# Attention and a two-layer MLP in one kernel: the second layer of batches 2 to 7 by seven block products per pair of tiles, with more key sums on TensorE

## The chip, the cores and the metric

The kernel runs on one core of a Trainium2 chip. The metric is the device time of one execution in microseconds (us). Engines are named as in the profile: PE is TensorE, PEld its weight loads, DVE is VectorE, ACT is ScalarE, POOL is GpSimd, and SP is SyncE, whose queue carries most DMAs. Each engine runs its own list of instructions in order, and waits at an instruction until what it needs is there.

## The reference

Eight batches of 12 heads, 448 tokens and 64 features go through attention with normalised queries and keys. The heads of a token are put side by side, which gives x with 3584 rows of 768, and two matrix products with a gelu between them follow.

```python
q_n, k_n = rmsnorm(q, g_q), rmsnorm(k, g_k)
scores = scale * np.matmul(q_n, k_n.transpose(0, 1, 3, 2))
scores = scores - np.max(scores, axis=-1, keepdims=True)
attn = np.exp(scores)
attn = attn / (np.sum(attn, axis=-1, keepdims=True) + 1e-09)
x = np.matmul(attn, v).transpose(0, 2, 1, 3).reshape(B * S, H * D)
h = x @ w_in                                   # 768 -> 2048
g = 0.5 * h * (1 + np.tanh(c * (h + 0.044715 * h * h * h)))
out = g @ w_out                                # 2048 -> 768
```

Inputs and outputs are float32; matmuls take bf16.

## The kernel before

**Work of a batch.** Queries and keys are loaded by SP in three chunks c of four heads (tiles `raw`). Their squares are made on ACT (L170) or POOL (L172), summed along the features on DVE (`total`, L177), and turned into reciprocal roots; `normed` (L279) multiplies, on POOL, six operations a batch. DMA transposes on SP (`dma_trans`) bring the result into `kT` and `qT`, and DVE applies the gains to `kT` (`gain`, L321).

An attention has 21 `unit`s: three chunks c times seven key tiles t. A unit is a round of four 64x64 matmuls with 448 columns (scores, L334) and an exp on ACT into the tile `ex` (L338). For the softmax's denominator the seven exps of a chunk are added on DVE in `key_sums` (L355 to L361: `es` = first two, then pairs `e2`, then `es` += `e2`), and the sum goes through one round with a matrix of ones on PE (`products(b, c, 0)`, L383). `added(b, c)` says up to which tile the exps are added first; all that are left would take a round each. `products(b, c, 1)` multiplies with v, seven rounds a chunk. `turned` (L392, two transposes of half a tile) and `recips` (L400 reciprocal, L401 transpose back) give `rb`, one over the denominators, and `quad_x` (L409) multiplies them with the product, into `xT`.

The first layer (`mm1_pair`, L599: 128x128 matmuls with 448 columns, 96 a batch, gelu on ACT at L612) writes `g`. The first two pairs of it begin, with the first two thirds of xT, at the end of the attention (the `m` steps), the rest follows. In the second layer (`mm2_quarters`, L443) a round is four 64x64 matmuls with 384 columns. Two products (a token tile of 128 by half of the 768 columns) share a PSUM pair `o`; each goes over the 16 blocks of the 2048 twice, in two phases p that use the opposite halves of the rows. Between the phases SP issues a `nop` (L452) that the next phase waits for, a "turn". Tiles are of 128 tokens of two batches together: an even batch gives three tiles, 96 rounds, an odd one four, 128 rounds. The four tiles of the last batch go through `quad_of_products` instead: the two tiles of a pair, the two halves of the 2048 and the two halves of the columns form 2x2 blocks, and seven products of block sums (L529, full 128x128 matmuls with 384 columns) give four blocks of output. The sums of g (`token_sums`, L517) and of the weights (`weight_sums`, L486) are made on DVE ahead of it.

**Order.** The order is written by hand and is the same on every engine's list. The first two batches are a string of steps (`first_two`). From then on the loop over b emits the first layer of batch b, with normalising of batch b+1 and loads and squares of batch b+2 put between its blocks by `plan` (`m1`), and then `attention(b + 1)`, whose string `steps` (one for even, one for odd) mixes U (a unit), d and a (rounds of the second layer of batch b; the copy that ends a product goes to DVE or ACT), A (key adds), s and x (`products`), t, r, q and m. I call such a stretch, first layer of b and attention of b+1, period b. The second layer's rounds come from a list that runs on from one period to the next, so each period has 112 of them. POOL's `mark` (`gpsimd_waits`, L756) copies one element of the last `es` of a batch; POOL's normalises of the next batch stand behind it.

**PSUM.** Four pairs of banks (s0, s1, t0, t1 in the names `s` and `t`) are handed out by `pair` and given back by `give`, first in, first out. A score, a product with v or ones, a first-layer pair and a second-layer product each take one.

**Buffers.** `rawqk` 4 of each, `sqp` 2 squares, `exq` 2 tiles of exps, `vb` 2 (v of even and of odd batches), `xp` 2, `op` 3 output tiles.

## Time and profile before

| what | value |
|---|---|
| median of 3 runs | 393.72 us (393.67 to 395.22) |
| the profiled execution | 394.05 us |
| its span in the profile | 392.1 us (1.95 us lie outside it) |
| mean granted clock of TensorE | 1.00 |
| second layer, L443 | 3072 matmuls, 768 rounds |
| scores L334, products L383 | 672 and 872 matmuls |
| first layer, L599 | 768 matmuls |
| POOL | 125.8 us busy in 105 instructions |

The span is the time from the profile's first instruction to its last. A row of the profile's groups has line, engine, operation, output and inputs with their shapes and a count, then busy time in us and the mean of one in ns, and behind a second bar the idle time of the engine ahead of them and what ended it. A row of the timeline has start, length, engine, line and operation; in square brackets the idle time before it. A row of the table by stretch has the stretch, its length and the busy time (and instructions) of PE, PEld, DVE, ACT and POOL, then PE's clock, DMA's share and GB/s.

### The profile page before, as it was taken

What the parts mean: (1) busy time and instruction counts of PE and PEld (TensorE: products, weight loads), DVE (VectorE), ACT (ScalarE), POOL (GpSimd) and SP (SyncE); (2) the same over time, 40 slices, a digit from 0 to 9 for tenths busy, and PEclk for the clock granted to TensorE, in tenths of its full rate; (3) what the DMA queues carried; (4) which work ended last, traced back from release to release, by engine and by line L of the source; (5) the groups of instructions that cost most, each with busy time, mean ns of one, the idle gap of its engine ahead of it and who ended that gap; (6) DMA issues with size and microseconds to landing.
All of it is one profiled execution on the core that took longest, in us unless ns stands there. A gap on an engine that the chain in (4) does not pass through costs nothing.

```text
span 392.1 us, 12742 instructions
## 1 busy us (share of the span) xinstructions
PE 384.0 (98%) x5649; PEld 245.3 (63%) x5649; DVE 271.9 (69%) x424; ACT 277.8 (71%) x349; POOL 125.8 (32%) x105
## 2 busy tenths in 40 slices
PE   7989999999999999999999999999999999999996
PEld 6455567855676558865666557865566556875554
DVE  4999539996699357963599456982579613999743
ACT  6995489567996589857898479857899349873410
POOL 5995501863304540083301840054400900000000
PEclk9999999999999999999999999999999999999999
DMA  8999997899752969249651859239632621120024
GB/s 266 255 233 222 204 186 153 303 185 260 150 135 56 249 81 225 55 98 272 106 144 42 192 137 205 65 86 230 118 75 46 132 47 43 43 57 27 0 61 101
DMA packets 65770, 54.36 MB, mean 139 GB/s; under 512 B 37428, under 2 KB 60852, under 8 KB 65716
## 3 DMA queue, kind: packets, MB, share of 16 engines
q1 hardware_dynamic: 53200, 41.33, 41.9%
q0 software_dynamic: 12128, 11.80, 19.4%
q8 instruction: 44, 0.72, 0.8%
q10 hardware_dynamic: 388, 0.43, 0.3%
q14 instruction: 10, 0.08, 0.1%
HBM read 45.61 MB, written 11.01 MB: 144 GB/s over the span
## 4 chain that ended last, share of the span: by engine, by line
PE 91%; ACT 5%; DVE 1%; DMA 1%; issue 0%; POOL 0%; ACTq 0%
PE s L599 21%; PE t L443 19%; PE t L599 15%; PE s L443 12%; PE s L383 6%; ACT ex L338 4%; PE s L334 4%; PE t L334 3%; PE t L383 3%; PE s L529 2%; PE t L529 2%; PE o L383 1%; PE tp L297 1%; DMA rawq<-in_q_dram 1%; PE hh L599 1%
## 5 line engine op out<-in xcount | busy, mean ns | idle before, releaser
L599 PEld LDWEIGHTS <-win 128*128 128x128 bf16 x768 | 74.4, 98 | 70.8 <-issue 2.6
L443 PEld LDWEIGHTS <-g 64*64 64x64 bf16 x3072 | 98.0, 107 | 32.8 <-SPq L452 2.9
L338 ACT ACTIVATE ex<-s,shift 128x896 bf16<-128x896 f32 x101 | 97.8, 1011 | 4.5 <-PE s L334 2.7
L443 PE MATMUL t<-wout,g 64*64 64x384 bf16 x1792 | 90.4, 323 | 0.0
L599 PE MATMUL s<-xT,win 128*128 128x448 bf16 x438 | 88.3, 353 | 0.0
L177 DVE TENSOR_REDUCE ss<-sq 128x14 f32<-128x896 f32 (+3 forms) x45 | 44.4, 997 | 48.1 <-ACT sq L170 42.9
L338 ACT ACTIVATE ex<-t,shift 128x896 bf16<-128x896 f32 x67 | 66.4, 1014 | 5.8 <-PE t L334 3.0
L612 ACT ACTIVATE g<-s 128x896 bf16<-128x896 f32 (+1 forms) x41 | 34.0, 835 | 48.5 <-PE s L599 48.5
L599 PE MATMUL t<-xT,win 128*128 128x448 bf16 x318 | 64.7, 353 | 0.0
L443 PE MATMUL s<-wout,g 64*64 64x384 bf16 x1280 | 64.6, 323 | 0.1
L612 ACT ACTIVATE g<-t 128x896 bf16<-128x896 f32 (+1 forms) x30 | 24.8, 829 | 26.3 <-PE t L599 26.3
L334 PE MATMUL s<-qT,kT 64*64 64x448 bf16 x404 | 37.6, 353 | 2.0 <-ACT ex L338 1.5
L756 POOL COPY mark<-es 1x1 bf16<-1x1 bf16 x5 | 0.9, 177 | 116.0 <-DVE es L357 116.0
L279 POOL TENSOR_TENSOR nrmk<-rawk,rinv 128x896 bf16<-128x896 f32 (+1 forms) x21 | 34.5, 1647 | 5.4 <-DVE o L246 5.4
L279 POOL TENSOR_TENSOR nrmq<-rawq,rinv 128x896 bf16<-128x896 f32 (+1 forms) x21 | 34.5, 1643 | 4.2 <-ACT rinv L209 2.9
L334 PEld LDWEIGHTS <-kT 64*64 64x64 bf16 x672 | 23.7, 106 | 14.7 <-issue 6.3
L172 POOL TENSOR_TENSOR sq<-rawq 128x896 f32<-128x896 f32 (+1 forms) x9 | 13.6, 1516 | 54.1 <-DVE ss L177 28.2
L383 PEld LDWEIGHTS <-vb 64*64 64x64 bf16 x672 | 22.9, 107 | 8.1 <-issue 0.3
L401 DVE STREAM_TRANSPOSE rb<-rc 128x896 f32<-128x896 f32 x24 | 26.7, 1112 | 0.8
L334 PE MATMUL t<-qT,kT 64*64 64x448 bf16 x268 | 24.1, 351 | 0.3 <-ACT ex L338 0.2
L360 DVE TENSOR_TENSOR e<-ex 128x896 bf16<-128x896 bf16 x33 | 20.0, 606 | 6.2 <-ACT ex L338 6.2
L383 PE MATMUL s<-ex,vb 64*64 64x448 bf16 x420 | 22.8, 349 | 0.0
(123 smaller groups left out, 404.2 us busy)
## 6 DMA issues: line engine op xcount, KB each, us to landing
rawk<-in_k_dram SPq DMA_DIRECT2D x23, 448.0 KB, 5.6
out_dram<-osb SPq DMA_DIRECT2D x52, 192.0 KB, 3.1
rawq<-in_q_dram SPq DMA_DIRECT2D x22, 448.0 KB, 4.8
vb<-in_v_dram POOLq DMA_DIRECT2D x8, 672.0 KB, 7.2
wout<-in_moe_w_out_dram POOLq DMA_DIRECT2D x2, 1536.0 KB, 23.4
win<-in_moe_w_in_dram POOLq DMA_DIRECT2D x6, 256.0 KB, 11.2
win<-in_moe_w_in_dram POOLq DMA_DIRECT2D x4, 384.0 KB, 13.4
rawq<-in_q_dram SPq DMA_DIRECT2D x3, 224.0 KB, 3.9
```

The source lines that it names most:

```text
L172: eng.tensor_mul(sq, raw, raw)
L177: nc.vector.reduce_sum(sss[b][:, c, "qk".index(n), hs, ts], squares(b, c, n, hs, ts), axis=AX.X)
L279: eng.tensor_mul(nrms[n, b, c][:, ts].rearrange("p t a d -> p a t d"), raws[n, b, c][:, :, ts], root[:, :, ts].to_broadcast([P, 2, m, D]),)
L334: nc.tensor.matmul(sc[r * R:(r + 1) * R, a, :S], kT[rs, c, t, r], qT[b][rs, c, :, r], start=True, stop=True,)
L338: nc.scalar.activation(ex[:, t], sc[:, :, :S], AF.Exp, scale=scale, bias=shift)
L360: nc.vector.tensor_add(e2, ex[:, t - 1], ex[:, t])
L383: nc.tensor.matmul(o[r][a * D:(a + 1) * D], vb[b % 2][rs, 2 * c + a, i] if what else ones[rs], es[i][rs, a], start=(i == 0), stop=(i == n ...
L401: nc.vector.transpose(rb.rearrange("p r s -> p (r s)"), rc.to_broadcast([128, 2 * S // 32, 32]))
L443: done = nc.tensor.matmul(o[c * R:(c + 1) * R, n, :HD], g[rs, f, i * 128 + c * R:i * 128 + (c + 1) * R], wout[rs, f, half * HD:(half + 1) ...
L529: nc.tensor.matmul(o[:, lo:hi], g_of(qd, m, f), w_of(m, f)[:, lo:hi], start=start and f == 0, stop=f == nh - 1, skip_group_check=True,)
L599: nc.tensor.matmul(h[j][:, :S] if type(h) is list else h[:, j, :S], win[:, c, f * 128:(f + 1) * 128], xT[b][:, c], start=(c == 0), stop=(c ...
L612: nc.scalar.activation(g[:, 2 * i + lo:2 * i + js[-1] + 1, (b % 2) * S:(b % 2 + 1) * S], h[:, lo:js[-1] + 1, :S], AF.Gelu_apprx_tanh)
```

## The change

**The second layer of batches 2 to 6** (`FAST = 2`) is made of block products over pairs of tiles, in rounds of four 64x64 matmuls as before. With A the two tiles by two halves of the 2048 (even and odd blocks of 128) and B the same halves by two halves of the columns, seven products m = "1" to "7" give the four output blocks; the sums they need share parts: `pair_sums` (two at a time, `wino_sum`, on DVE or POOL) and one in place in `g`; `tsum` holds four sums of the weights (`weight_sum`, eight operations in period 2, kept to the end). A product is 8 blocks long. In an odd batch both pairs of tiles go through a product side by side: seven products in two phases of eight, 112 rounds for 128. In an even batch one pair and a plain third tile make groups A to F: 88 rounds for 96. Products whose results go into two outputs stay in PSUM: P and R (later Q) are open at once, so a second-layer product holds two of the four PSUM pairs most of the time. `wino_done` copies a finished half into `oall4` (on DVE or ACT as the step says) or adds it to what is there (DVE). Between phases there is a turn as before. The last batch's four tiles go through `last_tiles` with the same sums: again 112 products, in the order of `TAIL`.

```diff
+    def wino_tiles(b):
+        return ((0, 1),) if b % 2 == 0 else ((3, 4), (5, 6))
+    def a_of(b, k, m, j):
+        t = wino_tiles(b)[k]
+        if m in "12":
+            return g[:, 2 * j + "12".index(m), t[0] * 128:(t[0] + 1) * 128]
+        if m == "4":
+            return g[:, 2 * j + 1, t[1] * 128:(t[1] + 1) * 128]
+        if m == "7":
+            return g[:, 2 * j, t[1] * 128:(t[1] + 1) * 128]
+        return pair_sums[:, wino_slots(b)[k], "536".index(m) // 2, j]
+    def wino_sum(b, k, i, part, eng):
...
+        dst, x, y, op = {
+            "1": (s1, g_part(t[1], 0, lo, n), g_part(t[1], 1, lo, n), ALU.add),
+            "2": (s2, s1, g_part(t[0], 0, lo, n), ALU.subtract),
+            "3": (g_part(t[1], 0, lo, n), g_part(t[0], 0, lo, n), g_part(t[1], 0, lo, n), ALU.subtract),
+            "4": (s1, g_part(t[0], 1, lo, n), s2, ALU.subtract),
+        }[i]
+        eng.tensor_tensor(dst, x, y, op=op)
+    def weight_sum(m, part, eng):
...
+        x, y, op = {"7": (b22, b12, ALU.subtract), "5": (b12, b11, ALU.subtract),
+                    "6": (own["7"], b11, ALU.add), "4": (b21, own["6"], ALU.subtract)}[m]
+        eng.tensor_tensor(own[m], x, y, op=op)
+    def wino_round(b, group, ph, j, copy):
...
+        for n in range(2):
+            lhs, rhs = two[n](j)
+            r = n ^ p
+            rs = slice(r * R, (r + 1) * R)
+            for c in range(2):
+                done = nc.tensor.matmul(
+                    o[c * R:(c + 1) * R, n, :HD], lhs[rs, c * R:(c + 1) * R], rhs[rs],
+                    start=firsts[n] and begins and j == 0, stop=swap == 1 and j == nh - 1,
+                    skip_group_check=True,
+                )
...
+            groups = [("1", "P", T, N), ("5", "R", T, N), ("6", "P", N, N), ("3", "R", N, T),
+                      ("7", "P", N, N), ("2", "Q", T, T), ("4", "P", N, T)]
...
+    TAIL = "1a 5a 6a 3a 7a 1b 4a 5b 6b 3b 7b 2a 4b 2b"
```

**Key sums.** `ADDED` lets more exps go to PE: batches 2 to 7 have 7 or more rounds of key sums where they had 3; with the first batches' that is 71 rounds for 50. The adds that are left are 81 on DVE (118 before) and 16 of the pairs `e2` on POOL ("Ap" in the strings). `turned` transposes a whole pair at once, 128x896, and `rb` takes the place of `st`.

```diff
-        return NT - 1 if b > 1 else (6, 4, 0)[c] if b else 0
+        return ADDED[b - 1][c] if b > 1 else (6, 4, 0)[c] if b else 0
...
-            nc.vector.tensor_add(e2, ex[:, t - 1], ex[:, t])
-            nc.vector.tensor_add(es, es, e2)
+            eng.tensor_add(e2, ex[:, t - 1], ex[:, t])
+            add(es, es, e2)
...
+        if whole:
+            nc.vector.transpose(st.rearrange("p r a b -> p (r a b)"), oas["o", 0][:, :, :S])
+            give(oas["o", 0])
+            return
...
-        rb = oas["rb"] = stp.tile([128, 2, S], F32, tag="rb", name="rb")
+        rb = oas["rb"] = oas["st"].rearrange("p r a b -> p (r a b)")
...
+    ADDED = {1: (6, 6, 6), 2: (5, 5, 3), 3: (5, 5, 4), 4: (6, 5, 3), 5: (5, 5, 4), 6: (6, 5, 3)}
```

**Order and buffers.** `plan`, `attention` and the loop's `m1` and `side` give way to one string for each period (`PERIODS`, played by `period`), in which every load, square, normalise, sum, gain and DMA transpose has its place too. Of period 6, from the last half pair of the first layer (h.7.1) to its end; U, d, a, A, s, x, t, r, q and m are as before, G a `wino_sum` (pair, sum, part, engine), gn a gain, dt a DMA transpose, V the load of v, w.e the mark:

```diff
+            "e.5 e.6 L.k.2 h.7.0 sq.k.2.P.0 to.k.0 L.q.1 G.0.1.0.V h.7.1 d sq.k.2.P.1 d2 L.q.2 dt.q.0 "
+            "d2 eE sq.q.1.P.0 d sq.q.1.P.1 d2 gn.2.V U to.k.1 U w.e sq.q.2.P U d dt.q.1 to.q.1 d "
+            "to.k.2 d2 G.0.1.1.V d to.q.2 d4 Ap d2 A d U d4 U G.0.2.2.V d Ap d U A d A d4 U A d3 A d2 "
+            "U Ap d3 G.0.4.0.V G.0.4.1.V d U d3 U d3 s.0 d t A d2 r G.0.3.2.P d U d dt.q.2 V A d2 Ap "
+            "d U d2 U d5 U d3 x.0 U A d2 q.0 Ap d U d4 Ap U d s.1 t d U A d A d5 a r U2 x.1 U d Ap Ap "
+            "d Ap q.1 d3 A d2 A a s.2 rE x.2 m.0 t r eG m.1 q.2 "
```

The steps L, sq and to in it would serve batch 8 and do nothing, as there are eight batches from 0 to 7. Sixteen rounds of batch 1 go over from period 1 to period 2; from then on odd periods have 112 rounds and even ones 88. `rawqk` has 3 buffers of each instead of 4, `sqp` is gone (`square_place`: squares lie in `tsum` for the first batches, then in a slot of the exps' ring `exq`), `xp` and `op` have 1, `vb` is a single tile. Some 24 half squares go from ACT to POOL. `released` and its two held tiles are gone.

**What that does to DVE's list.** From the attention of batch 6, before: one copy of a finished second-layer product (L457), key adds (L355 to L361), two half transposes and the reciprocals.

```order
L355 TENSOR_TENSOR es<-ex 128x896
L457 COPY osb<-t_885 128x768
L360 TENSOR_TENSOR e_5531<-ex 128x896
L361 TENSOR_TENSOR es<-es,e_5531 128x896
L360 TENSOR_TENSOR e_5542<-ex 128x896
L361 TENSOR_TENSOR es<-es,e_5542 128x896
L357 TENSOR_TENSOR es<-es,ex 128x896
L355 TENSOR_TENSOR es<-ex 128x896
L392 STREAM_TRANSPOSE st<-s_100 128x448 x2
L400 RECIPROCAL rc<-st 128x28
```

After, in the same attention from the first copy of a block product (L585) on; L556 is a sum of g, L395 to L400 are key adds, L197 sums squares.

```order
L585 COPY osb<-t_866 128x2x384
L556 TENSOR_TENSOR pair_sums<-pair_sums,g 128x1024
L395 TENSOR_TENSOR es<-ex 128x896
L197 TENSOR_REDUCE ss<-sq 128x14
L585 COPY osb<-s_97 128x2x384
L400 TENSOR_TENSOR es<-es 128x896
L556 TENSOR_TENSOR pair_sums<-g,pair_sums 128x512
L556 TENSOR_TENSOR pair_sums<-g,pair_sums 128x1024
L556 TENSOR_TENSOR pair_sums<-g,pair_sums 128x512
L399 TENSOR_TENSOR es<-ex 128x896
L400 TENSOR_TENSOR es<-es 128x896
L350 TENSOR_SCALAR kT<-kT,gcols 128x896
```

Fewer key adds stand between two transposes, and sums of g and copies or adds of block products stand there instead; a first L400 without an L399 adds a pair that POOL made.

**And to POOL's.** Before, the normalises of batch 7: the mark, which waits for the last `es` of batch 6, and behind it the six normalises.

```order
L756 COPY mark<-es 1x1
L279 TENSOR_TENSOR nrmq<-rawq,rinv 128x2x7x64
L279 TENSOR_TENSOR nrmk<-rawk,rinv 128x2x7x64
L279 TENSOR_TENSOR nrmq<-rawq,rinv 128x2x7x64
L279 TENSOR_TENSOR nrmk<-rawk,rinv 128x2x7x64
L279 TENSOR_TENSOR nrmq<-rawq,rinv 128x2x7x64
L279 TENSOR_TENSOR nrmk<-rawk,rinv 128x2x7x64
```

After, the end of batch 6's attention and the normalises of batch 7; L399 is the key add of a pair of exps.

```order
L556 TENSOR_TENSOR pair_sums<-pair_sums,g 128x512
L149 DMA vb<-in_v_dram 128x6x448
L399 TENSOR_TENSOR es<-ex 128x896 x2
L308 TENSOR_TENSOR nrmk<-rawk,rinv 128x2x7x64
L308 TENSOR_TENSOR nrmq<-rawq,rinv 128x2x7x64
L308 TENSOR_TENSOR nrmk<-rawk,rinv 128x2x7x64 x2
L308 TENSOR_TENSOR nrmq<-rawq,rinv 128x2x7x64 x2
L989 COPY mark<-es 1x1
L556 TENSOR_TENSOR g<-g 128x8x128
L149 DMA vb<-in_v_dram 128x6x448
L399 TENSOR_TENSOR es<-ex 128x896 x3
```

The mark has moved behind the normalises, and POOL has key adds and sums of g of its own between them.

529 lines of the change are left out of this document (298 added, 231 removed), and 70 rows, old and new, of tables (PERIODS, m2, steps).

## Prediction

> **What bounds the kernel now.** I read the page's busy line, slices and chain first, then the table by stretch, then the groups by form and the waits, and last the timeline of VectorE (DVE), ScalarE (ACT) and GpSimd (POOL) around one end of a batch. The page's first lines and the chain by engine:
>
> ```profile
> span 392.1 us, 12742 instructions
> PE 384.0 (98%) x5649; PEld 245.3 (63%) x5649; DVE 271.9 (69%) x424; ACT 277.8 (71%) x349; POOL 125.8 (32%) x105
> PE   7989999999999999999999999999999999999996
> PE 91%; ACT 5%; DVE 1%; DMA 1%; issue 0%; POOL 0%; ACTq 0%
> ```
>
> PE is busy in 98% of the span, and in all but three slices it is at nine tenths or more; 91% of the chain is its own work. So the time is a count of TensorE's matmuls times their pitch, plus its waits. Two whole periods (the first layer of one batch and the attention of the next), then one attention and the first layer behind it, in the table by stretch:
>
> ```profile
> 215.97:306.50 90.53, 90.53 (x1452) 58.30 (x1449) 61.02 (x88) 70.49 (x88) 28.66 (x21) 1.00 0.58 129
> ...
> 279.70:306.50 26.80, 26.80 (x628) 17.97 (x621) 21.30 (x33) 24.57 (x28) 3.15 (x5) 1.00 0.38 73
> 306.50:324.70 18.20, 18.20 (x100) 9.31 (x96) 5.39 (x7) 6.85 (x8) 8.05 (x5) 1.00 0.39 76
> ```
>
> The first number is the length, then PE, its weight loads, DVE, ACT, POOL. PE has no gap at a clock of 1.00, but the averages hide that DVE works unevenly: 21.30 of 26.80 us in an attention, 5.39 of 18.20 in a first layer. Its end of an attention is close: the last product that xT needs runs here, while PE does two early pairs (3.0 us from 306.50):
>
> ```profile
> 285.83 0.96 DVE L457 COPY osb<-t 128x768 f32<-128x768 f32 x1 [1.87 <-PE t L443]
> ...
> 308.26 1.09 DVE L409 TENSOR_TENSOR xT<-t,rb 128x896 bf16<-128x896 f32 x1
> ```
>
> It ends at 309.35, some 0.2 us before PE turns to it (306.50 + 3.03). DVE has little to spare there, though the share says 69%.
>
> **Second layer and key sums on PE.** Prices are in these pieces of the chain:
>
> ```profile
> 282.98 1.30 PE t L443 x32
> ...
> 293.11 1.32 PE s L383 x28
> ```
>
> A round is four matmuls. Eight second-layer rounds take 1.30 us, 0.1625 each; seven rounds of 448 columns take 1.32, 0.189 each. Batches 2 to 6 had 96, 128, 96, 128, 96 rounds and get 88, 112, 88, 112, 88: 56 fewer, 56 x 0.1625 = 9.10 us off the path. Batches 0 and 1 keep theirs, batch 7 keeps 112 large products. The key sums go from 50 rounds to 71: 21 x 0.189 = 3.97 us onto the path. The sum is **-5.13 us** while PE stays without gaps. That the change fails to do this is no case: the rounds are issued or not, and they are counted. Two periods of before hold 282 rounds of 448 columns (first layer counted in the same unit) and 224 of 384: 282 x 0.1892 + 224 x 0.1625 = 53.4 + 36.4 = 89.8 against 90.53 in the row above, so 0.39 us a period of small waits already hide in PE's busy time. I credit none of it as gain.
>
> **Turns.** Between the two phases of a product SP passes on a wait:
>
> ```profile
> PEld L443 <- SPq L452: 2.9, 10, 0.5
> ```
>
> It cost 2.9 us in ten waits in all. Afterwards there are as many turns or more, each covered by a score or key-sum round ahead of it; I take no change, bounds -1 to +1.
>
> **DVE's load.** Its prices:
>
> ```profile
> L357 DVE TENSOR_TENSOR es<-es,ex 128x896 bf16<-128x896 bf16 x32 | 20.0, 624 | 3.0
> L392 DVE STREAM_TRANSPOSE st<-t 128x448 f32<-128x448 f32 x28 | 16.5, 628 | 1.2 <-PE t L383 1.1
> L400 DVE RECIPROCAL rc<-st 128x28 f32<-128x28 f32 x24 | 7.9, 328 | 0.8
> L401 DVE STREAM_TRANSPOSE rb<-rc 128x896 f32<-128x896 f32 x24 | 26.7, 1112 | 0.8
> L409 DVE TENSOR_TENSOR xT<-s,rb 128x896 bf16<-128x896 f32 x15 | 16.3, 1087 | 1.2 <-PE s L383 0.8
> L457 DVE COPY osb<-t 128x768 f32<-128x768 f32 x6 | 5.7, 957 | 15.5 <-PE t L443 15.2 <-DMA rawq<-in_q_dram 0.3
> L517 DVE TENSOR_TENSOR asum<-g 128x512 bf16<-128x512 bf16 x16 | 5.5, 420 | 2.9 <-ACT g L612 2.9
> L517 DVE TENSOR_TENSOR asum<-g 128x1024 bf16<-128x1024 bf16 x2 | 1.3, 688 | 0.6 <-ACT g L612 0.6
> L177 DVE TENSOR_REDUCE ss<-sq 128x14 f32<-128x896 f32 x37 | 39.9, 1083 | 44.6 <-ACT sq L170 39.5 <-POOL sq L172 5.1
> 280.89 0.44 DVE L321 TENSOR_SCALAR kT<-kT,gcols 128x896 bf16<-128x896 bf16 x1
> ```
>
> For batch 6's attention before, from the copy at 285.83 to 309.35: 18 key adds of 0.62, one copy, six half transposes of 0.63, three each of 0.33, 1.11 and 1.09: 23.5 us of work in 23.52 us. So sums of mean durations are a fair measure of DVE when it runs without stop. After the change the list from the first second-layer product (ready behind 16 rounds and three scores, 16 x 0.1625 + 3 x 0.189 = 3.2 us) to the last xT is: 12 key adds 7.4; four pair sums of 512 and two of 1024, 1.7 + 1.4; five copies or adds of 768 columns 4.8; a reduce 1.1; a gain 0.4; three whole transposes at the price of L401 (1.11 against 2 x 0.63) 3.3; three reciprocals 1.0; three L401 3.3; three L409 3.3: 27.7 us. It ends at 3.2 + 27.7 = 30.9 us. PE has 112 rounds, 49 of 448 columns and the two early pairs: 18.2 + 9.3 + 3.0 = 30.5. So PE waits some 0.4 us. In an even batch's period the list has 11 key adds (6.8), sums 1.5, three copies of 384 at half of L457 (1.5), two adds of 384 (1.1, half of L409), two of 768 (1.9) and the same 10.9: 23.7 from 3.2 on, 26.9 against PE's 88 x 0.1625 + 49 x 0.189 + 3.0 = 26.6: 0.3 late. Taken 0.35 in each of the five periods of batches 2 to 6: **+1.75 us**; bounds 0 (work in a better place) and 1.0 each. The period of batch 2 also holds eight weight sums, at this price 7.6 us, half of them in a first layer, where DVE idles; the ten at the end of before go:
>
> ```profile
> L486 DVE TENSOR_TENSOR wsum<-wout 128x1536 bf16<-128x1536 bf16 x10 | 8.8, 951 | 0.0
> ```
>
> **Accumulators.** Two second-layer products are open at once, so two of four PSUM pairs are left for scores, v products and key sums, and a score waits for the exp of two before it. ACT's pitch and its present waits:
>
> ```profile
> 326.73 3.70 ACT L338 ACTIVATE ex<-s,shift 128x896 bf16<-128x896 f32 x4
> ACT ex L338 <- PE t L334: 3.0, 7, 0.6
> ```
>
> Exps come every 0.9 us; units stand mostly 0.7 us or more apart, so a pair can come 0.2 to 0.6 late. DVE, which is the later one, uses that time too, so it isn't counted twice: 0 taken, bound 0.8 in each of the three even periods. ACT itself gets lighter (some 24 half squares go to POOL, at 0.57 in the row below), so it isn't the next bound.
>
> ```profile
> L170 ACT ACTIVATE sq<-rawq 128x448 f32<-128x448 f32 x22 | 11.9, 570 | 0.6 <-DMA rawq<-in_q_dram 0.6
> L279 POOL TENSOR_TENSOR nrmk<-rawk,rinv 128x896 bf16<-128x896 f32 x20 | 33.7, 1687 | 5.4 <-DVE o L246 5.4
> POOL mark L756 <- DVE es L357: 116.0, 5, 23.7
> ```
>
> **POOL.** It takes sixteen key adds (at L279's 1.69 us), those squares and some pair sums; at 125.8 us busy before, it has room. The question is what it does beside DVE. Before, POOL stood 116.0 us behind the mark, until the last key add was through. Afterwards the mark stands behind the normalises of most periods, so they start beside the last key adds. What a POOL operation does to one of DVE's shows here; DVE's gains alone normally take 0.44:
>
> ```profile
> 311.08 1.68 POOL L279 TENSOR_TENSOR nrmq<-rawq,rinv 128x896 bf16<-128x896 f32 x1
> 312.73 1.83 POOL L279 TENSOR_TENSOR nrmk<-rawk,rinv 128x896 bf16<-128x896 f32 x1
> ...
> 311.50 1.51 DVE L321 TENSOR_SCALAR kT<-kT,gcols 128x896 bf16<-128x896 bf16 x1 [2.16 <-DMA kT<-nrmk]
> 314.05 0.76 DVE L321 TENSOR_SCALAR kT<-kT,gcols 128x896 bf16<-128x896 bf16 x1 [1.04 <-DMA kT<-nrmk]
> ```
>
> Both gains ended 0.25 us after the POOL operation in whose time they fell (312.76, 314.56). They lost 1.07 and 0.32, a mean of 0.70 us a meeting. Not everything suffers: this pair of DVE ran at its usual speed inside POOL's normalises of 304.48 to 309.46:
>
> ```profile
> 305.47 1.17 DVE L392 STREAM_TRANSPOSE st<-s 128x448 f32<-128x448 f32 x2
> 307.04 1.11 DVE L401 STREAM_TRANSPOSE rb<-rc 128x896 f32<-128x896 f32 x1
> ```
>
> Whether a key add suffers, no row shows: before, none runs beside POOL. The bounds are none and every POOL operation of the attention (some five a period, 25 x 0.70 = 17.5 us in five periods); I take the price of one meeting on the path in all, **+0.7**, since in the order DVE's transposes, reduces and reads of PSUM stand beside a good part of POOL's work. [...]
>
> **V and the tail.** One v buffer instead of two lets the load start only behind the last v product of the batch before, on POOL's queue:
>
> ```profile
> DMA to landing us min/median/max: 6.5/7.2/28.1
> ```
>
> In an even period it is issued behind a pair sum; 7.2 us later is 13 to 15 us, against the first v product at 13.3. I take 0, bounds 0 and 1 a period in two periods. Likewise three raw buffers for four, and squares that take a slot of the exp tiles: a load or an exp can come late by the part of an attention that isn't spare; 0 taken, and a place in the upper end of the range. The last four tiles keep 112 products; their sums of weights are done earlier, 0 taken, bounds -0.5 and +0.5.
>
> **The sum.** 393.72 - 5.13 + 1.75 + 0.7 = 391.0 us. The profiled run took 394.05 (392.1 of span and 1.95 outside), 0.33 above the median; by it the sum is 391.4.
>
> **Rivals.** *A meeting in every period.* If key adds suffer as the gains do, and one meeting falls on the path in each of the five periods, 5 x 0.70 = 3.5 replaces the 0.7: 393.8, no change. For it: DVE's list is as long as the period, so each loss goes on to PE. Against: the lists end only 0.3 to 0.4 us late, so one operation less on DVE in a period takes much of a loss back. Chance 0.24.
> *POOL and DVE hold each other off (the other side).* Two meetings a period on the path, one of a key add or pair sum with a POOL key add or square, one of the last key adds with the next batch's normalises, which the mark no longer holds back: 10 x 0.70 = 7.0, 393.72 - 5.13 + 1.75 + 7.0 = 397.3. It decides from (1.75 + x 0.70 = 5.13) five meetings on. For it: the gains' rows, and the trace of before, which keeps the two apart with its 116.0 us wait. Against: the transposes beside POOL at full speed. It shows first at the key sums ahead of a transpose and at the end of an attention. Chance 0.24. [...]
>
> **How the numbers follow.** 0.5% is 2.0 us, about what a measurement of this kernel can tell from no change. My forecast, 391.0, is faster; chance 0.52, with 388.6 (no lateness at all) to 391.7. It, and the two rivals, give the chances 0.52, 0.24, 0.24. The low end, 387.5, is 388.6 less half of the 0.39 us x 6 that hides before; the high end, 397.5, takes in both rivals' prices; more than ten meetings, some 1 in 8, are left out above it, and less below 387.5.
>
> **What would show it.** PE busy should fall to some 379 (384.0 - 5.1), DVE stay near 270 (37 key adds fewer, but more sums and adds out of PSUM), and POOL rise to some 185 (125.8 + 16 x 1.69 + 24 halves of that + a dozen pair sums of one each). Right: waits of PE for xT at the start of a first layer of about 0.4 us each, and key adds near 0.62. The first rival: one key add a period of 1.3 us or more. The second: the mean of key adds well above 0.62 and PE gaps over 1 us per period ahead of the key sums or the first layer. Wrong in another way: PE waits for exps or a pair of PSUM, or for v, each over 1 us a period.

## The result, and the profile after

The changed kernel takes 409.41 us (median of 4 runs, 407.24 to 410.9) against 394.29 (393.67 to 395.22) of the kernel before, measured beside it: a ratio of 1.037 with a 95% interval of 1.034 to 1.041. It is slower by 15 us; the forecast was 391.0 and its upper end 397.5. The profiled execution took 409.1 us. The page's first lines, answering to those of before:

```profile
span 407.3 us, 12496 instructions
PE 386.4 (95%) x5509; PEld 242.6 (60%) x5509; DVE 279.9 (69%) x406; ACT 264.8 (65%) x325; POOL 198.1 (49%) x153
PE   7989999999899999999989999999998999999795
PEclk9999999999999999999999999999999999999989
```

PE has 140 matmuls fewer (5649 to 5509: 56 rounds off and 21 on, of four each), as counted, but the share of its busy time went from 98% to 95%, and three things are new: eights in the middle, a hole near the end, and a clock below full there. So the question is which waits came in. (The forecast expected PE at some 379 us busy, DVE at 270 and POOL at 185. PE's busy time isn't work alone: in batch 7's attention below it is 24.93 us for 23.57 by count.) The table by stretch holds the six attentions of batches 2 to 7, cut where PE leaves one first layer and enters the next. Before, the first and the last of the six:

```profile
98.17:125.45 27.28, 27.28 (x630) 19.14 (x629) 22.29 (x34) 24.73 (x28) 5.84 (x6) 1.00 0.53 118
...
324.76:351.69 26.93, 26.93 (x629) 21.50 (x629) 20.95 (x32) 24.10 (x26) 0.00 (x0) 1.00 0.18 47
```

And after, those of batches 2, 4 and 7:

```profile
99.08:128.51 29.43, 27.45 (x629) 18.64 (x629) 23.31 (x33) 24.77 (x29) 15.08 (x12) 1.00 0.53 114
...
194.60:225.72 31.12, 28.59 (x646) 21.47 (x645) 26.17 (x39) 25.19 (x29) 9.32 (x7) 1.00 0.51 72
...
336.38:361.62 25.24, 24.93 (x549) 18.03 (x548) 20.01 (x31) 22.94 (x25) 8.66 (x5) 1.00 0.50 80
```

The first two numbers are length and busy PE. This table sets each length against its count of rounds, at the prediction's 0.1625 and 0.189 us:

| attention of batch | 2 | 3 | 4 | 5 | 6 | 7 | all |
|---|---|---|---|---|---|---|---|
| before: length | 27.28 | 26.93 | 27.07 | 26.93 | 27.07 | 26.93 | 162.2 |
| before: by count | 26.71 | 26.71 | 26.71 | 26.71 | 26.71 | 26.71 | 160.3 |
| after: length | 29.43 | 28.79 | 31.12 | 25.23 | 30.63 | 25.24 | 170.4 |
| after: by count | 26.71 | 26.20 | 27.47 | 23.57 | 27.47 | 23.57 | 155.0 |
| after: late | 2.7 | 2.6 | 3.7 | 1.7 | 3.2 | 1.7 | 15.5 |

By count the attentions lose 5.3 us, as forecast. They grew by 8.2, since PE came 15.5 us late in them where it had been 1.9 late. Batches 5 and 7, with 88 rounds, are the only ones that got shorter. The rest of the 15.2 us of span: 4.65 in the last product of the kernel (18.55 to 23.20), 0.9 up to the first layer of batch 1, 0.8 in that of batch 3, 0.6 behind the last matmul; what makes these three was not looked into. PE's waits by what released it:

```profile
PE t L683 <- DVE pair_sums L556: 3.0, 1, 3.0
PE t L625 <- SPq L633: 2.1, 2, 1.3
PE s L363 <- ACT ex L367: 2.0, 5, 0.6
PE s L625 <- issue: 1.7, 1, 1.7
PE s L363 <- DVE osb L508: 1.4, 1, 1.4
...
PE t L739 <- DVE xT L457: 0.2, 1, 0.2
```

The third row is nearly old: before the change PE waited 1.5 us, four times, for ACT's exps. The others are new. So there isn't one cause but several, each once or twice. The wait on which the forecast spent its largest term, for xT at the start of a first layer, is the last line: 0.2 us in all.

**The last product.** DVE and POOL share the sums of g there. The timeline of DVE, of POOL, and PE's first round behind them:

```profile
380.57 0.76 DVE L556 TENSOR_TENSOR pair_sums<-g 128x512 bf16<-128x512 bf16 x2 [16.02 <-ACT g L752]
381.85 1.38 DVE L556 TENSOR_TENSOR g<-g 128x512 bf16<-128x512 bf16 x1
383.15 1.37 DVE L556 TENSOR_TENSOR pair_sums<-pair_sums,g 128x512 bf16<-128x512 bf16 x1
...
384.44 2.67 DVE L556 TENSOR_TENSOR pair_sums<-g,pair_sums 128x512 bf16<-128x512 bf16 x2
```
```profile
381.48 1.47 POOL L556 TENSOR_TENSOR pair_sums<-pair_sums,g 128x512 bf16<-128x512 bf16 x1 [7.30 <-DVE pair_sums L556]
382.91 3.58 POOL L556 TENSOR_TENSOR g<-g 128x512 bf16<-128x512 bf16 x2
```
```profile
386.83 2.37 PE L683 MATMUL t<-wout,pair_sums 128*128 128x384 bf16 x8 [2.97 <-DVE pair_sums L556]
```

A sum of 512 columns took 0.38 us on DVE before POOL began (two in 0.76), and 1.38, 1.37 and 2.33 beside POOL; the last is the first of the two in 2.67, the second took 0.41 when POOL was done. The first of those ended 0.28 us behind the POOL operation in whose time it fell (383.23, 382.95), as the gains of before did. PE then waits 2.97 us, and what follows costs as well. The table by stretch in steps of 2 us:

```profile
386.00:388.00 2.00, 1.17 (x5) 0.61 (x6) 1.11 (x2) 0.00 (x0) 0.49 (x1) 0.81 0.00 0
388.00:390.00 2.00, 2.00 (x8) 0.95 (x7) 0.56 (x1) 0.00 (x0) 0.00 (x0) 0.50 0.00 0
390.00:392.00 2.00, 2.00 (x12) 1.15 (x11) 0.56 (x1) 0.00 (x0) 0.00 (x0) 0.83 0.00 0
```

The granted clock, third from the end, falls to 0.50 behind the pause: (0.19 + 0.50 + 0.17) x 2.0 = 1.7 us of PE's work are lost. 2.97 + 1.7 makes the 4.65. The second part isn't always paid: seven of the later traces have the same pause of 2.97, and in four of them (E3, E5, E6, E9) the clock stays at 1.00 and the last product takes 21.53.

**The turns.** In the odd batches SP issues the stores of a finished product, and the next turn's `nop` stands behind them in its queue. SP's row and the round that waited, in batch 6's attention:

```profile
311.37 3.32 SPq L479 DMA_DIRECT2D out_dram<-osb  x4
```
```profile
314.80 1.49 PE L625 MATMUL t<-tsum,g 64*64 64x384 bf16 x32 [1.28 <-SPq L633]
```

Four issues take SP 3.32 us, until 314.69, and PE goes on at 314.80. Batch 4's attention has the same wait, 0.83 us.

**Two pauses without a releaser**, in the attentions of batches 4 and 6, both while the load of v for that batch runs on POOL's queue and a DMA transpose of q beside it:

```profile
208.70 0.52 PE L625 MATMUL s<-wout,pair_sums 64*64 64x384 bf16 x8 [1.70 <-issue]
...
301.59 0.35 PE L363 MATMUL s<-qT,kT 64*64 64x448 bf16 x1 [0.87 <-issue]
```

"issue" says that PE waited for nothing that the profile shows. From 204 to 206 us, ahead of the first, the DMA table has one packet of instructions with 9.7% of 16 engines' time, 0.097 x 16 x 2 = 3.1 us of one engine (most packets of this kind in this trace take 0.9 to 1.4):

```profile
q8 instruction: 1, 0.02, 9.7%
```

**The attention of batch 2.** A copy of a finished product on DVE stands behind sums of squares that POOL makes late, and a score waits for the PSUM pair that this copy frees. POOL in turn waits for a load of k. POOL's row, then DVE's:

```profile
100.73 3.32 POOL L189 TENSOR_TENSOR sq<-rawk 128x896 f32<-128x896 f32 x2 [1.64 <-DMA rawk<-in_k_dram]
```
```profile
104.08 2.08 DVE L197 TENSOR_REDUCE ss<-sq 128x14 f32<-128x896 f32 x2 [3.75 <-POOL sq L189]
...
109.34 0.95 DVE L508 COPY osb<-s 128x768 f32<-128x768 f32 x1
```
```profile
110.34 0.38 PE L363 MATMUL s<-qT,kT 64*64 64x448 bf16 x4 [1.38 <-DVE osb L508]
```

**The attention of batch 3.** One key add on DVE met one on POOL, and took 2.30 us where the other 19 of its form take 0.61 on the mean (13.9 less 2.3, in the table below). PE then waits 0.42 us for a sum of g behind it, and 0.43 for an exp:

```profile
152.65 2.30 DVE L395 TENSOR_TENSOR es<-ex 128x896 bf16<-128x896 bf16 x1
```
```profile
152.56 1.91 POOL L399 TENSOR_TENSOR es<-ex 128x896 bf16<-128x896 bf16 x1
```

**The even batches**, whose second layer, of 88 rounds, runs in the attentions of batches 5 and 7. ACT's exps there stand end to end at their pitch of 0.89 us, and a score waits for the exp of two before it. ACT, then PE, in batch 7's attention:

```profile
340.14 1.01 ACT L367 ACTIVATE ex<-s,shift 128x896 bf16<-128x896 f32 x1
341.03 1.02 ACT L367 ACTIVATE ex<-t,shift 128x896 bf16<-128x896 f32 x1
```
```profile
341.20 0.38 PE L363 MATMUL s<-qT,kT 64*64 64x448 bf16 x4
342.10 0.38 PE L363 MATMUL t<-qT,kT 64*64 64x448 bf16 x4
```

The score at 341.20 goes into pair s and starts 0.05 us behind the end of the exp that read s (340.14 + 1.01 = 341.15); the next, at 342.10, likewise behind 342.05. Between them stand two or three rounds of the second layer and no more, 0.19 + 3 x 0.1625 = 0.68 us of work, so PE takes ACT's pitch, 0.90.

Against these the table by form shows what did not happen: 33 DVE key adds of one form kept 0.62 us, their price of before. They hardly had a chance to suffer: of DVE's 81 key adds five overlap an operation of POOL at all, and one of the five is the 2.30 above. The meetings fall on other work. Of the 19 gains, ten stand beside POOL, at 0.93 us on the mean, and nine don't, at 0.46. All told 18 DVE operations took over 0.15 us longer than the median of their form, 14.6 us together (before: three, 2.1 us). PE pays for this only where it waits for DVE just then, above all at the end.

```profile
L400 DVE TENSOR_TENSOR es<-es 128x896 bf16<-128x896 bf16 x33 | 20.5, 622 | 2.9 <-POOL es L399 2.0
L395 DVE TENSOR_TENSOR es<-ex 128x896 bf16<-128x896 bf16 x20 | 13.9, 693 | 3.3 <-ACT ex L367 2.3 <-issue 0.4 <-PE t L429 0.3
L399 POOL TENSOR_TENSOR es<-ex 128x896 bf16<-128x896 bf16 x16 | 30.2, 1891 | 62.6 <-ACT ex L367 53.2 <-DVE es L400 9.4
```

### The profile page after: what moved, and what is told of

It reads as the page before. It is cut to its first block, busy times and chain, and to the rows that moved or that the text cites. A ratio compares the mean times of both kernels' runs of the same rounds, so it can differ in the third digit from the quotient of the medians.

```text
span 407.3 us, 12496 instructions
## 1 busy us (share of the span) xinstructions
PE 386.4 (95%) x5509; PEld 242.6 (60%) x5509; DVE 279.9 (69%) x406; ACT 264.8 (65%) x325; POOL 198.1 (49%) x153
## 5 line engine op out<-in xcount | busy, mean ns | idle before, releaser
L739 PE MATMUL t<-xT,win 128*128 128x448 bf16 x342 | 69.1, 353 | 0.2 <-DVE xT L457 0.2
L399 POOL TENSOR_TENSOR es<-ex 128x896 bf16<-128x896 bf16 x16 | 30.2, 1891 | 62.6 <-ACT ex L367 53.2
L625 PEld LDWEIGHTS <-g 64*64 64x64 bf16 x1280 | 50.3, 107 | 14.9 <-SPq L633 3.9
L197 DVE TENSOR_REDUCE ss<-sq 128x14 f32<-128x896 f32 (+1 forms) x34 | 34.3, 1022 | 25.7 <-ACT sq L187 16.5
L625 PE MATMUL t<-wout,g 64*64 64x384 bf16 x576 | 42.7, 324 | 0.0
L494 PE MATMUL s<-wout,g 64*64 64x384 bf16 x768 | 38.5, 323 | 0.7 <-SPq L503 0.6
L625 PEld LDWEIGHTS <-pair_sums 64*64 64x64 bf16 x672 | 28.6, 106 | 10.7 <-issue 3.3
L494 PEld LDWEIGHTS <-g 64*64 64x64 bf16 x896 | 28.2, 107 | 10.8 <-issue 1.4
L625 PE MATMUL t<-tsum,g 64*64 64x384 bf16 x448 | 29.3, 323 | 2.2 <-SPq L633 2.1
L556 DVE TENSOR_TENSOR pair_sums<-g 128x512 bf16<-128x512 bf16 (+1 forms) x12 | 6.1, 526 | 31.3 <-ACT g L752 31.3
L449 DVE STREAM_TRANSPOSE st<-rc 128x896 f32<-128x896 f32 x24 | 26.7, 1111 | 0.8
```

The costliest lines, as they stand in the source:

```text
L197: nc.vector.reduce_sum(sss[b][:, c, "qk".index(n), hs, ts], sq, axis=AX.X)
L399: eng.tensor_add(e2, ex[:, t - 1], ex[:, t])
L449: nc.vector.transpose(rb.rearrange("p r s -> p (r s)"), rc.to_broadcast([128, 2 * S // 32, 32]))
L494: done = nc.tensor.matmul(o[c * R:(c + 1) * R, n, :HD], g[rs, f, i * 128 + c * R:i * 128 + (c + 1) * R], wout[rs, f, half * HD:(half + 1) ...
L625: done = nc.tensor.matmul(o[c * R:(c + 1) * R, n, :HD], lhs[rs, c * R:(c + 1) * R], rhs[rs], start=firsts[n] and begins and j == 0, stop=s ...
L739: nc.tensor.matmul(h[j][:, :S] if type(h) is list else h[:, j, :S], win[:, c, f * 128:(f + 1) * 128], xT[b][:, c], start=(c == 0), stop=(c ...
```

## The experiments

The theory after this reading: each wait has its own place and cause, so each can be taken off alone, and what they cost adds up. The rival: the kernel is simply late as a whole (too much on DVE, or block products that bring nothing), so a wait taken off comes back at the next place. All times below are medians, with the ratio to the kernel before on the same chip; the runs of one kernel lie 2 to 6 us apart, so a difference of 1 us between two medians says little.

**E1, the last product's sums on DVE alone.**

```diff
-            "l.0 l.1 e.2 e.3 e.4 e.5 e.6 h.7.0 h.7.1 G.0.1.1.V G.1.1.0.P G.0.1.0.P G.1.1.1.V "
-            "G.1.2.1.P G.0.3.1.P G.0.2.2.V G.0.3.0.V G.1.3.2.P G.1.2.0.V "
+            "l.0 l.1 e.2 e.3 e.4 e.5 e.6 h.7.0 h.7.1 G.0.1.0.V G.1.1.0.V "
+            "G.0.1.1.V G.0.2.2.V G.0.3.2.V "
...
+            if step == "3a":
+                for i, part in (("1", 1), ("2", 2), ("3", 2)):
+                    wino_sum(b, 1, i, part, nc.vector)
```

> All sums of g for the last batch are on DVE, none on POOL; those of the second pair of tiles stand behind the first pair's last sum. Theory 1 (a DVE sum that meets a POOL sum waits for its end): DVE's 512-wide sums go back from 1.4 to 0.42 us, PE's gap of 2.97 us in the tail and the drop of its clock to 0.70 behind it vanish, the tail falls from 23.2 to some 18.6 us, the whole from 409.4 to some 404.8. Rival (the new order of the seven products needs its sums before DVE can make them, whoever makes them): the gap stays over 1.5 us, and moving POOL's five sums to DVE makes it longer, 409 to 411.

403.95 us (402.13 to 406.27), ratio 1.025 [1.020, 1.030]. The last product takes 18.78 us in place of 23.20. DVE's sums for the first pair of tiles have their own pace, 0.39 for 512 columns; those for the second come later, where DVE idled:

```profile
380.69 0.78 DVE L556 TENSOR_TENSOR pair_sums<-g,pair_sums 128x512 bf16<-128x512 bf16 x2
```

That DVE's sums lose time beside POOL's is shown by the rows (1.38 and 1.37 us before this edit, 0.39 with it), and this edit takes 4.4 us off the last product. It changes two things, the engine and the place of the second pair's sums; it doesn't part them.

**E2, stores issued behind the next turn.** They are kept in a list and issued once the next `nop` is.

```diff
-                    store(b, x[stored])
+                    waiting.append((b, x[stored]))
...
+            stored_now()
```

> In the block products the stores of a finished tile are issued behind the next turn on SP's queue instead of ahead of it. Theory (a turn stands behind four stores on SP, so PE waits for SP): PE's waits for SP of 0.83 and 1.28 us late in the attentions of batches 4 and 6 vanish, those two attentions get 1.0 to 1.5 us shorter, the whole 2 to 3 us (about 407). Rival (the turn itself is late, or PE would then wait for exps): PE waits there for something else and the time stays within 0.7 us of 409.4.

405.24 us (403.34 to 406.69), ratio 1.027 [1.023, 1.031]. No round of the block products waits for SP any more, and the attentions of batches 4 and 6 fall from 31.12 and 30.63 to 29.37 and 28.74. Of the two pauses without a releaser 0.39 and 0.60 were left in this run, so some of the gain is theirs. The edit moves the stores of block products only: in E8, which has it too, a turn in batch 3's attention still waits 1.24 us, behind stores of batch 1's last plain product.

**E3, the transposes of q.2 (`dt.q.2`) moved right behind those of k.2 in periods 3 and 5**, to take them away from the load of v.

> In the periods of batches 3 and 5 the last DMA transpose of queries is issued some 4 us sooner, ahead of two turns on SP's queue, so that it runs ahead of the load of v. Theory (PE's stalls of 1.70 and 0.87 us around 208 and 301 us, which wait for nothing that the profile shows, come from instructions that are fetched late beside the DMA transposes and the load of v): they vanish or shrink below 0.4 and the whole falls by 1.5 to 3 us. Rival (they come from something in PE's or DVE's list): they stay where they are, and the time with them.

408.25 us (406.4 to 411.34), ratio 1.035 [1.030, 1.040]: 1.2 us less, which is within the spread. The two pauses are gone, but a turn now stands behind three transposes, whose issues take SP from 287.51 to 293.32 us, the last alone 2.71, and PE waits 2.33 us for it:

```profile
PE s L625 <- SPq L633: 2.8, 2, 2.3
```

So the place where the transposes stand is no free choice: the queue that carries the turns has to stay clear.

**E4, all sixteen key adds of POOL on DVE.**

```diff
-                key_sums(n, *units[added_to], nc.gpsimd)
+                key_sums(n, *units[added_to], nc.vector)
```

> The sixteen key adds of POOL are made by DVE at the same places of the order. Theory 1 (POOL's operations cost DVE more by shutting it out, some 0.7 us a meeting, than they save): DVE's sums and gains lose less, and the whole gets 2 to 5 us faster. Theory 2 (DVE is the engine that is late, so 16 x 0.62 = 10 us more on it come through in part): 2 to 6 us slower. If neither is near a limit: within 1 us.

414.23 us (412.05 to 416.94), ratio 1.050 [1.045, 1.055]: worse by 4.8 us. Now PE waits for key adds on DVE, 4.5 us in all, and the attentions of batches 5 and 7 take 26.85. Theory 2 holds. Giving these adds to POOL pays here, in spite of the few meetings.

```profile
PE t L429 <- DVE es L400: 1.7, 3, 0.8
PE s L429 <- DVE es L397: 1.5, 1, 1.5
PE s L429 <- DVE es L400: 1.3, 2, 0.8
```

**E5, no load of v for batches 4 and 6** (they multiply with the v of the batch before, so the output is another).

```diff
-                load_v(n, 0, HP)
+                if n not in (4, 6):
+                    load_v(n, 0, HP)
```

> The loads of v for batches 4 and 6 are left out (those batches multiply with the v that is there). Theory (instructions for PE are fetched late beside the load of v and the DMA transposes): PE's stalls without a releaser around 208 and 301 us stay below 0.2 us, the attentions of batches 4 and 6 get about 1 us shorter each, the whole 1 to 3 us. Rival (another cause): stalls of 0.3 to 2 us stay.

406.32 us (403.87 to 408.82), ratio 1.030 [1.024, 1.036]. Both pauses are gone, and the attentions of batches 4 and 6 take 29.44 and 29.62. That the load of v brings them on fits, but isn't shown: the traces of E3, E6, E7, E8 and E11 load v and have no such pause in these attentions either, in E10 one of 2.32 us began when the load had landed, and E4 has one of 1.08 in batch 3's attention that began 1.7 us after that batch's v had landed. The late packet of instructions is better borne out. In the traces of the changed kernel and of the runs there are fifteen of these pauses, and each ends 1.3 to 1.7 us after one such packet was through; ahead of the four longest (1.70, 2.21, 2.25 and 2.32 us) the packet took 3.11, 3.41, 2.74 and 1.70 us.

**E6, the key sums as before** (all seven exps of a chunk added on DVE and POOL, three rounds on PE a period).

```diff
-    ADDED = {1: (6, 6, 6), 2: (5, 5, 3), 3: (5, 5, 4), 4: (6, 5, 3), 5: (5, 5, 4), 6: (6, 5, 3)}
+    ADDED = {b: (6, 6, 6) for b in range(1, 7)}
```

> The key sums of batches 2 to 7 go back to one round of PE a chunk, 19 rounds fewer than in the changed kernel (3.6 us of PE), with 26 key adds more, mostly on DVE (16 us). Theory (DVE is near its limit, so adds on it come through at a third to a half, as in the run with the sixteen adds moved): 2 to 5 us slower than the changed kernel's 409.4. Rival (DVE still has room in most places): 2 to 4 us faster.

431.43 us (429.64 to 433.42), ratio 1.094 [1.088, 1.099], far outside both expectations. The rounds taken off are 21, not 19, all in batches 3 to 7: batch 2 has three in the changed kernel too. PE waits 20.5 us for last key adds:

```profile
PE s L429 <- DVE es L397: 14.2, 8, 5.4
PE t L429 <- DVE es L397: 6.3, 6, 2.8
```

The new order places the adds of a chunk late, because few are meant to be left, so this run does not price the key sums alone. It shows that the 21 rounds and the order belong together.

**E7, the second layer of batches 2 to 6 as before**, in the new order (`FAST = 8`, the sums of g taken out, the rounds spread over the same places); the last batch keeps its block products.

```diff
-    FAST = 2
+    FAST = 8
```

> Batches 2 to 6 keep the old second layer (56 rounds more, one product open at a time, no sums of g for them); all else as changed: key sums, POOL's adds, buffers, order, the last batch. If the block products bring their 9.1 us of PE and cost little in waits: 409.4 + 7 to 9 = 417 or so. If their waits (pairs of PSUM, turns behind stores, sums) eat them up: attentions of batches 3 to 7 at their counted length plus 0.3 to 0.6, as before the change, and the whole between 405 and 411.

413.67 us (412.07 to 417.82), ratio 1.051 [1.043, 1.059], between the two expectations. The attentions take 28.92, 32.07, 26.44, 32.27 and 26.24 us from batch 3 on. So the block products do bring something, 413.67 - 409.41 = 4.3 us, and 9.1 by count. Set against its count of rounds as in the table, E7 is 11.0 us late in the six attentions (175.1 against 164.1), where the changed kernel is 15.5. So most of the lateness is there without the products, in what E7 leaves as it is: the order, the key sums, POOL's work and the single buffers. Some 4.5 us of it come with them.

**E8, three waits off at once**: E1, E2, and in batch 2's attention the late copy put on ACT (`d2 U to.q.2 d8 U` becomes `d2 U d a d6 to.q.2 U`).

> The changed kernel with three repairs: the last batch's sums on DVE, stores behind the turns, and in the attention of batch 2 the copy of the finished product on ACT at once, with a DVE reduce behind it. If the waits found add up: 409.4 - 4.9 (tail) - 2.6 (turns of batches 4 and 6) - 2.4 (attention of batch 2) = 399.5, from 398 to 401.5. If a wait that goes only makes room for the next: 402 or more.

404.02 us (401.9 to 405.23), ratio 1.023 [1.019, 1.028]: 0.1 us from E1 alone. In the profiled execution the last product is repaired (18.78), but batch 2's attention takes 31.01: the copy is out of the way, yet a score waits 1.43 us for an exp, which itself waits 1.42 for DVE's sums of squares to free a slot of the exps' ring, and the clock falls behind it (0.56 and 0.59 in two steps of 2 us). In batch 6's a sum of g on DVE (L556) is late instead, behind a gain that waited 1.84 us for a DMA transpose; a second such sum took 1.73 beside POOL. In batch 2 the rival is right: the wait came back at another place. The one in batch 6 isn't in E10 and E12, which have the same edit of the stores.

**E9, squares of batch 3 also in `tsum`**, so that they take no slot of the exps' ring.

```diff
-        if b < 3:
+        if b < 4:
```

> The squares of batch 3, made during the attention of batch 2, lie in the weight sums' tile (not yet written then) and not in a slot of the exps' ring. Theory (an exp of the second chunk waits 2.07 us for DVE's sums of those squares, and PE for that exp): ACT's wait for those sums vanishes there, the attention of batch 2 falls from 29.4 to 27 or 27.5 us, the whole by 2 to 2.5 us. Rival (PE waits there for DVE's copy of a finished product, which stands behind the same sums): PE's wait of 1.38 us for that copy stays and the gain is under 0.7 us.

407.78 us (407.04 to 408.86), ratio 1.034 [1.032, 1.037]. ACT's wait for the sums of squares is gone. Batch 2's attention falls from 29.43 to 28.69, and the wait for the copy is 0.69 in place of 1.38, but the edit isn't what did that: in E10, which has it too, they are 29.34 and 1.34, and in E1, without it, 28.31 and 0.29. The wait goes with POOL's squares of k, which wait for their load: they began 1.65 us behind the start of the attention in the changed kernel and 0.51, 0.91 and 1.56 behind it in E1, E9 and E10. So the rival is right that PE waits for the copy, and the copy is as late as the load.

**E10, four waits off**: E1, E2, E9, and the POOL key add that met DVE's in batch 3's attention put on DVE (`Ap A d3 U2` becomes `A2 d3 U2`).

> Four repairs together: the last batch's sums on DVE, stores behind the turns, squares of batch 3 out of the exps' ring, and one key add in the attention of batch 3 moved from POOL to DVE (beside it a key add of DVE took 2.30 us). If the waits found add up: 409.4 - 4.9 - 2.6 - 2.4 - 1.2 = 398.3, from 396.5 to 400.5 with the stalls of late instructions. If a wait that goes makes room for the next: 402 or more. Faster than the kernel before in neither case.

401.91 us (398.18 to 403.44), ratio 1.018 [1.012, 1.024], between the two expectations. Batch 3's attention takes 28.21 (28.79), batch 6's 28.31 (30.63), the last product 18.77 (23.20). Batch 2's, 29.34, is what it was. Batch 4's takes 32.40 in the profiled execution: a pause without a releaser of 2.32 us, and behind it the clock, down to 0.50.

**E11, the second layer and the key sums as before, with the repairs**: E7, E6, E1, E2 and E9 together.

> Old second layer for batches 2 to 6, one round of key sums a chunk, and the repairs of the last batch and of the squares; what is left of the change is the order, POOL's adds and squares, and the single buffers. PE's rounds are those of the kernel before. If the block products and the key sums carry the loss: 394 to 396. If the order and the buffers carry a good part: 413.7 - 3.6 - 4.9 - 2.4 = 402.8, from 400 to 405.

427.57 us (425.21 to 427.96), ratio 1.083 [1.079, 1.087]. Neither expectation held: PE waits 15.1 us for last key adds, as in E6. With the key sums back on DVE this order loses these 15 us, whatever else was repaired here.

**E12, E10 without the loads of v for batches 4 and 6, and with E8's copy on ACT** (output as in E5).

> The four repairs of the run with four waits off (last batch's sums on DVE, stores issued behind the turn, squares of batches 2 and 3 in tsum, one key add of the second attention on DVE), and two things more: the loads of v for batches 4 and 6 are left out (their values stay those of the earlier batch, so the output is not the reference's), and in the attention of batch 2 the last copy of a pass goes to ACT. By my account, which gives each wait its own place: 409.4 less 4.9 for the tail, 2.6 for the turns, 2.4 for the attention of batch 2, 1.2 for that of batch 3, 2.9 for the two pauses of late instructions (1.9 and 1.0): about 395.3 us, with 394 to 398 as its range; attentions of batches 4 and 6 at 28.0 or less, of batches 5 and 7 unchanged at 25.2. Rival, that the waits are one lateness that moves to the next wait when one is taken off: no better than 399 us, with new waits for DVE or ACT of over 0.5 us in the attentions of batches 2, 4 and 6.

398.3 us (397.11 to 399.2), ratio 1.011 [1.008, 1.014]: 0.3 above the range of the account and below the rival's 399. The attentions take 29.07, 27.69, 28.09, 25.24, 28.09 and 25.23 us; that of batch 4:

```profile
193.10:221.19 28.09, 28.09 (x645) 21.21 (x644) 26.33 (x39) 24.96 (x29) 7.96 (x6) 1.00 0.25 55
```

In batches 4 and 6 the account holds: 0.6 us late each by count (28.09 against 27.47), where it was 3.7 and 3.2. Batch 2's attention is where it fails: no score waits for the copy or the slot any more, but the key adds stand where they stood, behind the same late sums of squares (the last of these adds ends 12.5 us after the attention's start, 12.8 in the changed kernel), and PE, now there sooner, waits 1.60 us for the key sum instead. DVE, then PE:

```profile
110.94 0.62 DVE L397 TENSOR_TENSOR es<-es,ex 128x896 bf16<-128x896 bf16 x1
```
```profile
111.61 0.38 PE L429 MATMUL t<-es,ones 64*64 64x448 bf16 x4 [1.60 <-DVE es L397]
```

So the copy, the slot and the key adds, counted apart, are one lateness: that of the squares, and of the load of k ahead of them.

Of the 15.1 us, 409.41 - 398.3 = 11.1 go when these waits are taken off together, and part of them only by leaving loads out, which is no repair; the theory's sum was 14, and the 3 that lack are mostly batch 2's, where the rival is right. The time still isn't below that of the kernel before. What is left is 8.4 us of lateness in the attentions (163.4 of length, 155.0 by count): 2.4 and 1.5 in those of batches 2 and 3, 0.6 in those of 4 and 6, and 1.7 in those of 5 and 7, which no run made shorter. None of the twelve beats the kernel before.

## Why the prediction was wrong

The forecast was 2.7 us of gain, and the kernel lost 15.1. The step that failed is not the count of rounds but the sum of the waits: +2.45 us was put down for them, in two places, and the new waits elsewhere were taken at 0 one by one. They came to 13.5 us in the attentions (15.5 late in place of 1.9) and 4.65 in the last product.

- **The count, -5.13 us: right.** 140 matmuls fewer, and 5.3 us less in the attentions by count. E7 measures what the block products keep of their 9.10: 4.3.
- **"DVE's load", +1.75: did not come about as described.** No first layer of the changed kernel waited for xT by more than 0.2 us. DVE's list was long enough to be near the bound, but it was late in the middle, at single places, not at the end of an attention.
- **"Turns ... I take no change, bounds -1 to +1": failed.** I counted the turns and not what stands ahead of them in SP's queue. The stores of the odd batches stand there; 1.28 and 0.83 us of PE's waits in the rows above are theirs, and E2, which only moves them, gains 4.2 us with part of it from the pauses.
- **"0 taken, bounds -0.5 and +0.5" for the tail: failed, and the largest single error.** The forecast's own second rival has DVE losing time beside POOL, but I looked for it at key adds only. The sums of g of the last batch are the one place where both engines work on the same list with PE waiting for each: 4.4 us by E1, of which about 1.7 is the clock, in the traces where it fell.
- **"Meetings", +0.7, and the second rival's ten: DVE does lose time beside POOL (gains at 0.93 us for 0.46, sums of g at 1.38 for 0.38), the place and number were wrong.** The key adds, which both rivals priced, hardly met POOL (five of 81) and so keep 0.62 us in the mean; in the attentions one meeting counted, in batch 3's (E10, with that add on DVE: 0.6 us less there). The meetings fell on gains, weight sums and sums of g, and hurt PE at the end. The rival's total, 397.3, is on the right side but for a reason that accounts for about 5 of the 15 us.
- **"Accumulators ... 0 taken, bound 0.8 in each of the three even periods": mis-sized.** 1.7 us late in the attentions of batches 5 and 7, of which about 1.0 is ACT's pitch by the rows shown, the rest key sums a little late. I took it to be hidden by DVE's lateness, which wasn't there. That it is ACT's pitch was read and not tried: in E7, with one product open at a time and more rounds between the scores, these two attentions are still 1.6 and 1.4 late, there partly behind key sums and a copy on DVE.
- **"V ... 0 taken, bounds 0 and 1 a period": failed, in another way than was feared.** PE did not wait for v, though the loads took 10.9 and 10.6 us to land there and not 7.2. But PE paused without a releaser while they ran, for 1.70 and 0.87 us, the first beyond the bound; E5 fits that the load brings this on and doesn't show it.
- **"Three raw buffers for four, and squares that take a slot of the exp tiles ... 0 taken": failed**, 1.38 us of wait and more in batch 2's attention, which is 2.7 late. The slot alone gains nothing (E9, E10). The load of k is what is late, and SP's own waits, after and before, say that a load now stands until a normalise of k has freed its buffer:

```profile
SPq L126 <- POOL nrmk L308: 12.7, 8, 2.8
```
```profile
SPq L125 <- POOL nrmk L279: 0.2, 1, 0.2
```

That is read and not tried: no run gives the fourth buffer back.

What these steps share: each took a new wait at nothing because the engine or queue in question had time to spare on the whole, and none looked at what stands ahead of the awaited instruction in its queue at that place.

## What to carry to other kernels

Where one engine is busy for 98% of the span, a change that takes 5 us of its work away also takes away the slack that the others lived on; look at each place where it waits for a queue, and list everything that stands ahead of the awaited instruction in that queue (here stores ahead of a turn, reduces ahead of a copy, a normalise ahead of a load), since a sum of each engine's load doesn't show it. Give two engines of which one slows the other (here DVE's sums of g, 1.38 us beside POOL for 0.38 alone) different stretches, not halves of one urgent list, and look first at the end of the kernel, where nothing covers them. When two or three waits lie close together, look for what they all stand behind before you repair them one by one. A pause of the matmul engine can cost more than its length: behind the 2.97 us in the last product the granted clock was 0.50 for 3.41 us, which cost 1.7 us more.

## What was unexpected of the hardware

**The clock behind short pauses.** In E10 the pause without a releaser of 2.32 us was followed by this (granted clock in the third column from the end):

```profile
208.00:210.00 2.00, 1.24 (x20) 0.79 (x24) 0.04 (x1) 0.00 (x0) 0.00 (x0) 0.79 0.00 0
210.00:212.00 2.00, 2.00 (x30) 1.23 (x26) 0.98 (x2) 1.01 (x1) 0.28 (x1) 0.50 0.03 8
212.00:214.00 2.00, 2.00 (x44) 1.45 (x40) 1.69 (x3) 0.84 (x1) 1.60 (x1) 0.86 0.00 0
```

(0.21 + 0.50 + 0.14) x 2.0 = 1.7 us lost, as in the last product. There the clock was 0.50 from 387.25 to 390.66, 3.41 us; here 1.7 us lost at 0.50 make some 3.4 too. Shorter pauses did it too: 1.2 to 1.4 us with another 0.5 to 0.6 a little later, in three runs (E2, E5 and E8, batch 2's attention, mean clock there 0.94, 0.95 and 0.94). But the same pair of pauses in the changed kernel (1.38 and 0.59) did not, nor did 1.70 in its batch 4's attention, nor 2.25 in E9's. So such a wait cost itself, or itself and 1.7 us more; what decides between the two isn't shown.

**Pauses behind a packet of instructions.** PE's pauses without a releaser vary between runs of kernels that differ elsewhere, from none to 2.3 us, and each of the fifteen ends 1.3 to 1.7 us after a packet of instructions was through. They are gone in both runs without the load of v, and in five with it. That PE stands there because its instructions come late is my reading; no row shows it. What holds the packet up is open.
